# Two buffers instead of three for five small tags, in a set-attention and MoE kernel on one core

## The chip, the cores and the metric

The kernel runs on one core of a Trainium2 chip. The metric is the device time of one execution in microseconds (us), as the median of several runs. The engines that matter here are TensorE (PE, with its weight loads shown apart as PEld), ScalarE (ACT), VectorE (DVE) and SyncE's DMA queue (SPq).

## The reference

```python
def _attn_ref(x, inducing):            # x: 4 x 12480 x 128, inducing: 32 x 128
    def mab(q, kv):
        s = scale * (q @ kv.transpose(0, 2, 1))
        s = s - s.max(-1, keepdims=True)
        a = np.exp(s)
        a /= a.sum(-1, keepdims=True) + 1e-09
        return a @ kv
    h = mab(I, x)                      # I: inducing, once for each batch
    return mab(x, h)

def _moe_ref(x, w_in, w_out):          # 49920 tokens, 128 -> 2048 -> 128
    h = x @ w_in
    g = h * (1.0 / (1.0 + np.exp(-1.702 * h)))
    return g @ w_out
```

The output of the attention goes straight into the two products of the feed-forward part. The weights are handed over in 64-bit form and are decoded on the chip at the start.

## The kernel before

The work on the tokens is cut into blocks of 512. For one block the attention weights of the tokens over the 32 rows of `h` are turned and split into a high and a low part and stacked in a tile `st` (128 x 512). `h` times `w_in`, split the same way, stands in tiles `hw`. One matmul of `st` against 128 columns of `hw` so gives 128 hidden rows of a block: this is the **first product** (`hidden`, from line 1337). It is done for two chunks of hidden rows at a time, into a pair of PSUM banks `ph`. ScalarE applies the gated function to both banks in one instruction and writes `g`; ScalarE again, or VectorE by a copy, writes the rounded part `hi`, and VectorE writes the rest `lo = g - hi` (`first`, from line 1351). The **second product** (`second`, from line 1366) takes three matmuls for each chunk, and adds them up in a bank `pso`:

```python
            pe_.matmul(o, wlc, hi[:, c, :], start=(ch == 0), stop=False)
            pe_.matmul(o, whc, lo[:, c, :], start=False, stop=False)
            pe_.matmul(o, whc, hi[:, c, :], start=False, stop=last)
```

A group `i` is thus two matmuls of the first product and six of the second, all with 128 x 128 weights and 512 moving columns. A block has 8 groups, and its `pso` goes out through `ob` after the 48th matmul. There are 98 blocks' worth of such work, the last two with fewer columns (tile `left`).

The main loop (from line 1488) lays the matmuls out in one order, which is fixed when the program is built: `begin_group` decides by modelled clocks of the engines whether the next thing for TensorE is a pair of first products or three second products of an earlier group; up to 18 of those lie between the two. Pieces of the attention of later batches (`attention`, `second_softmax`, `weights_of`) are put in between, as their matmuls into banks `pa`.

The small tiles of the attention come from the pool `psm`, which has three buffers for a tag unless the tag names another number. Five tags are of interest: `mx` and `rs` (128 x 7 numbers, made once for each batch by `new_batch`, the running maxima and sums), `nmx`, `mx1` and `rs1` (128 x 1, made once for each batch, and `nmx` and `mx1` twice in the start-up, by `maximum`).

Where the tiles lie: pools are laid behind one another in each partition's memory, in the order in which they are opened, and each buffer begins at a multiple of 32 bytes. The pools for `xt`, `s1`, `e`, `aT`, `st`, `left` and `hw` are opened before `psm`, and those for `whole`/`wh`, `wl`, `g`, `hi`, `lo` and `ob` after it. The addresses in a partition, as the program of the kernel before has them:

```
tile              first address   modulo 256   part
xt                        26560          192   moving operand of the attention's products
st (4 buffers)            94016           64   moving operand of the first product
left                     102208           64   the same, for the last blocks
hw (4 buffers)           103744           64   weights of the first product
mx, rs, mx1              120128     64 to 64   (three buffers of 32 bytes for each tag)
nmx, rs1                 120544   224 to 160   (the same)
wh (2 buffers)           122848          224   weights of the second product
wl                       131040          224   weights of the second product
g (3 buffers)            139232          224
hi (9 buffers)           151520          224   moving operand of the second product
lo (9 buffers)           188384          224   moving operand of the second product
ob (2 buffers)           225248          224
```

The buffers of `st`, `hw`, `wh`, `hi` and `lo` are 2048 or 4096 bytes long and their chunks are 512 or 2048 bytes apart, so that every operand of a tag has the residue that the table gives.

Of the kernel before, what the change touches and what calls it, by code (L numbers as in the profile page):

```python
# [9 lines left out]
F32 = mybir.dt.float32  # L10
# [7 lines left out]
P = 128  # L18
# [214 lines left out]
def set_attention_then_moe(ctx: ExitStack, tc, xT, x, indT, w_in, w_out, outT):  # L233
# [67 lines left out]
    NS = len(sups)  # L301
# [11 lines left out]
    psm = ctx.enter_context(tc.tile_pool(name="psm", bufs=3))  # L313
# [49 lines left out]
    def full(some):  # L363

        free = range(len(held) - EB, len(held) - EB + sum(s < NS - 1 for s in some))
        return any(k >= 0 and not held[k] for k in free)
# [12 lines left out]
    def until(eng, t):  # L379

        while eng.t < t and not late[0]:
            yield

    def room():

        while min(dve.t, act.t) > pe_.t + ROOM and not late[0]:
            yield

    def hop(n=4):

        for _ in range(n):
            yield

    def load_xT(b, s, t=None):
        t0, g, w = sups[s]
        if t is not None:
            pass
        elif g == G:
            t = px.tile([P, SUP], F32, tag="xt", name="xt")
        else:  # L400
            t = px.tile([P, g * w], F32, tag="xt_last", name="xt_last", bufs=1)
        sp.dma_start(t[:, 0:g * w], xT[:, b * N + t0:b * N + t0 + g * w])
        xts[b, s] = t
# [24 lines left out]

    def new_batch(b):
        a = SimpleNamespace(b=b, s1={}, aTs={}, col={s: k for k, s in enumerate(EARLY + LATE if b == 0 else range(NS))})  # L430
        a.mx = psm.tile([P, NS], F32, tag="mx", name="mx")
        a.rs = psm.tile([P, NS], F32, tag="rs", name="rs")
        dve.memset(a.mx, -3.0e38)
        dve.memset(a.rs, 0.0)
        return a
# [45 lines left out]
    def max_scaled(pa):  # L481

        row = psm.tile([P, M], F32, tag="row", name="row", bufs=1)
        dve.tensor_reduce(
            row, pa[:, 0:P].rearrange("p (g m) -> p m g", g=G), axis=AX.X, op=ALU.max
        )
        dve.tensor_mul(row, row, mine)
        nmx = psm.tile([P, 1], F32, tag="nmx", name="nmx")
        dve.tensor_reduce(nmx, row, axis=AX.X, op=ALU.add)
        return nmx  # L490

# [94 lines left out]
    def pairs(some):  # L586
        some = list(some)
        return [some[k:k + 2] for k in range(0, len(some), 2)]

    def attention(b):  # L590

        for s in range(XB):
            yield from until(pe_, clocks.free("xt", XB))
            load_xT(b, s)
            yield
        a = new_batch(b)
        for pair in pairs(range(NS)):
            while full(pair):
                yield
            yield from until(  # L600
                pe_, max(clocks.ready(*[xts[b, s] for s in pair]), clocks.free("pa", 2, 2))
            )
            pas = [first_products(a, s) for s in pair]
            yield
            for s, pa in zip(pair, pas):
                if s + XB < NS:
                    load_xT(b, s + XB)
                yield from until(dve, clocks.ready(pa))
                yield from room()
                first_copy(a, s, pa, dve)  # L610
                yield from hop(HOPS[0])
            yield from hop(HOPS[1])
        mx1 = psm.tile([P, 1], F32, tag="mx1", name="mx1")
        dve.tensor_reduce(mx1, a.mx, axis=AX.X, op=ALU.max)
        yield from hop(HOPS[2])
        pa = max_everywhere(mx1)
        yield
        nmx = max_scaled(pa)
        yield from hop(HOPS[3])
        yield from until(act, clocks.ready(nmx))  # L620
        yield from deep()
        for s in range(4):
            first_exponential(a, s, nmx)
        yield
        pa = ps_a.tile([P, 512], F32, tag="pa", name="pa")
        i = 0
        xns = {}
        for s in range(XB):
            yield from until(pe_, clocks.free("xt", XB))
            xns[s] = load_x(b, s)  # L630
            yield
        for some in ((0, 1), (2, 3), tuple(range(4, NS))):
            if some[0] == 2:
                yield from deep()
                for r in range(4, NS):
                    first_exponential(a, r, nmx)
                yield
            for s in some:
                yield from until(dve, clocks.ready(a.s1[s][0]))
                yield from room()  # L640
                aT_of(a, s)
                yield from hop(HOPS[4])
            yield from until(pe_, clocks.ready(*[t for s in some for t in (a.aTs[s], xns[s])]))
            for s in some:
                i = weigh(a, pa[:, 0:P], s, xns[s], i, blocks(range(NS)))
            yield from hop(HOPS[5])
            for s in some:
                if s + XB < NS - 1:
                    xns[s + XB] = load_x(b, s + XB)
                elif s == 2:  # L650
                    t = pt.tile([P, TOK // P, P], F32, tag="t", name="xn_last")
                    xns[NS - 1] = load_x(b, NS - 1, t)
                if s != NS - 1 and s > 1:
                    again(b, s - 2)
                yield from hop(HOPS[6])
        hu = psm.tile([P, P], F32, tag="hu", name="hu", bufs=1)
        dve.tensor_copy(hu, pa[:, 0:P])
        rs1 = psm.tile([P, 1], F32, tag="rs1", name="rs1")
        dve.tensor_reduce(rs1, a.rs, axis=AX.X, op=ALU.add)
        rsb = spread(rs1)  # L660
        yield from hop(HOPS[7])
        pa = sums(hu, rsb)
        yield
        normalised(b, pa, denominators(pa[:, P:P + M]))
        yield from hop(HOPS[8])
# [164 lines left out]
    def start(pf, pw):  # L830
        a = new_batch(0)
# [170 lines left out]

        def maximum(n):
            yield dve, [a.mx], has(*[("max", s) for s in (EARLY + LATE)[:n]])
            mx1 = psm.tile([P, 1], F32, tag="mx1", name="mx1")
            dve.tensor_reduce(mx1, a.mx[:, 0:n], axis=AX.X, op=ALU.max)
            tag = "ph" if n == NS else "pa"
            yield pe_, [mx1], bank(tag)
            pa = ps_h.tile([P, 2, 512], F32, tag="ph", name="ph")[:, 0] if n == NS else None
            pa = max_everywhere(mx1, pa)  # L1010
            hold(tag)
            yield dve, [pa], None
            nmxs[n] = max_scaled(pa)
            hold(tag, -1)
            done.add(("nmx", n))
# [59 lines left out]
        def joining():  # L1075

            yield dve, lambda: [nmxs[ES], nmxs[NS]], has(("nmx", ES), ("nmx", NS), *[("exp", s) for s in EARLY])
            less = psm.tile([P, 1], F32, tag="less", name="less", bufs=1)
            dve.tensor_sub(less, nmxs[NS], nmxs[ES])
            rs1 = psm.tile([P, 1], F32, tag="rs1", name="rs1")  # L1080
            rs2 = psm.tile([P, 1], F32, tag="rs2", name="rs2", bufs=1)
            dve.tensor_reduce(rs1, a.rs[:, 0:ES], axis=AX.X, op=ALU.add)
            yield act, [less], None
            act.activation(less, less, AF.Exp)
            yield dve, [less, a.rs], has(*[("exp", s) for s in range(NS)])
            dve.tensor_reduce(rs2, a.rs[:, ES:NS], axis=AX.X, op=ALU.add)
            dve.scalar_tensor_tensor(rs1, rs1, less, rs2, op0=ALU.mult, op1=ALU.add)
            rsb = spread(rs1)
            yield pe_, [rsb], bank("pa")
            pa = ps_a.tile([P, 512], F32, tag="pa", name="pa")  # L1090
            pe_.matmul(pa[:, 0:M], rsb, rep2[:, 0:M], start=True, stop=True)
            hold("pa")
            yield dve, [pa], None
            den = denominators(pa[:, 0:M])
            hold("pa", -1)
            yield dve, [h12, less], has(*[("weighed", s) for s in range(NS)])
            hu = psm.tile([P, P], F32, tag="hu", name="hu", bufs=1)
            dve.tensor_scalar(hu, h12[:, 0:P], less, None, op0=ALU.mult)
            dve.tensor_add(hu, hu, h12[:, P:2 * P])
            yield pe_, [hu], bank("pa")  # L1100
            pa = ps_a.tile([P, 512], F32, tag="pa", name="pa")
            pe_.matmul(pa[:, 0:P], hu, rep2, start=True, stop=True)
            hold("pa")
            yield dve, [pa], None
            normalised(0, pa, den)
            hold("pa", -1)
            done.add("h")
# [447 lines left out]
```

## Time and profile before

| | before |
|---|---|
| median of 3 runs | 1568.65 us (1568.57 to 1568.71) |
| span of the profiled execution | 1566.7 us |
| TensorE busy | 1558.6 us (99%) |
| ScalarE busy | 1353.6 us (86%) |
| VectorE busy | 1309.7 us (84%) |

The span goes from the first instruction to the last one on the core; the runs' own time, with what lies around the span, is 2.0 us longer. The matmuls are pipelined: each is listed with some 0.39 us, and the next starts before it ends. What TensorE needs for one is therefore read from the distance between two starts, not from its listed length.

### The profile page before, as it was taken

How to read it: one execution, taken by the hardware profiler on the slowest of the kernel's cores; microseconds unless marked ns; L12 is line 12 of the kernel's file. 1: busy time of each engine (PE TensorE's matmuls, PEld its weight loads, DVE VectorE, ACT ScalarE, POOL GpSimd, SP SyncE). 2: the span in 40 equal slices, each digit the busy share in tenths (PEclk: the TensorE clock that was granted, in tenths of full speed). 3: DMA queues.
4: the chain of work that ended last, by engine and by line, in shares of the span. 5: the costliest groups of instructions: out<-in, count | busy, mean ns of one | idle time of the engine just before them, and what ended most of it. 6: DMA issues, size and time to landing. Idle time of an engine off the chain costs nothing.

```text
span 1566.7 us, 21731 instructions
## 1 busy us (share of the span) xinstructions
PE 1558.6 (99%) x7736; PEld 1228.8 (78%) x7736; DVE 1309.7 (84%) x1521; ACT 1353.6 (86%) x1552; POOL 4.5 (0%) x9
## 2 busy tenths in 40 slices
PE   9999999999999999999999999999999999999999
PEld 6577778877778788787787878788778888888887
DVE  7888888888888868888788887888878888888886
ACT  5999899898998898887999889888899998888884
POOL 1000000000000000000000000000000000000000
PEclk9999999999999999999999999999999999999999
DMA  8210257722151087211023119330201101101100
GB/s 328 78 44 22 58 192 125 208 62 83 29 197 41 29 150 196 73 48 61 27 91 137 38 53 220 101 95 28 68 21 40 48 24 38 48 23 39 47 23 22
DMA packets 83849, 127.53 MB, mean 81 GB/s; under 512 B 12320, under 2 KB 50848, under 8 KB 77856
## 3 DMA queue, kind: packets, MB, share of 16 engines
q1 hardware_dynamic: 83600, 126.05, 28.5%
q8 instruction: 63, 1.03, 0.3%
q14 instruction: 42, 0.34, 0.1%
q10 hardware_dynamic: 144, 0.10, 0.0%
HBM read 72.11 MB, written 25.56 MB: 62 GB/s over the span
## 4 chain that ended last, share of the span: by engine, by line
PE 97%; DMA 2%; DVE 1%; SPq 0%; issue 0%; ACT 0%; DVEq 0%
PE pso L171 69%; PE ph L171 24%; PE pa L171 4%; DMA xt<-in_xT 1%; PE h L171 0%; DVE whole L171 0%; DVE tmp L171 0%; SPq L186 0%; PE spun L1237 0%; DMA hw<-tl 0%; DVE e L171 0%; DVE s L171 0%; ACT hi L171 0%; DVE sm L171 0%; DVE tl L171 0%
## 5 line engine op out<-in xcount | busy, mean ns | idle before, releaser
L171 DVE TENSOR_TENSOR lo<-g,hi 128x1024 fp32r<-128x1024 f32 x776 | 938.4, 1217 | 155.2 <-ACT hi L171 141.7
L171 ACT ACTIVATE g<-ph 128x1024 f32<-128x1024 f32 (+1 forms) x784 | 809.8, 1036 | 177.7 <-PE ph L171 84.4
L171 PE MATMUL pso<-lo,wh 128*128 128x512 f32 (+1 forms) x1552 | 608.1, 392 | 0.0
L171 PE MATMUL pso<-hi,wl 128*128 128x512 f32 (+1 forms) x1552 | 607.6, 392 | 0.0
L171 PE MATMUL pso<-hi,wh 128*128 128x512 f32 (+1 forms) x1552 | 606.9, 391 | 0.0
L171 ACT ACTIVATE hi<-ph 128x1024 fp32r<-128x1024 f32 (+1 forms) x483 | 499.1, 1033 | 0.0
L171 PE MATMUL ph<-st,hw 128*128 128x512 f32 x1536 | 484.8, 400 | 1.4 <-ACT g L171 1.2
L171 PEld LDWEIGHTS pso<-hi,wl 128*128 128x128 f32 x1552 | 291.2, 188 | 75.7 <-issue 4.2
L171 PEld LDWEIGHTS ph<-st,hw 128*128 128x128 f32 x1536 | 285.5, 188 | 80.3 <-issue 9.0
L171 PEld LDWEIGHTS pso<-lo,wh 128*128 128x128 f32 x1552 | 291.4, 188 | 67.2 <-issue 0.2
L171 PEld LDWEIGHTS pso<-hi,wh 128*128 128x128 f32 x1552 | 291.3, 188 | 63.2
L171 DVE CAST hi<-g 128x1024 fp32r<-128x1024 f32 (+1 forms) x293 | 200.2, 683 | 76.7 <-ACT g L171 76.3
L171 ACT COPY ob<-pso 128x512 f32<-128x512 f32 (+1 forms) x98 | 59.3, 606 | 11.1 <-PE pso L171 11.1
L171 ACT ACT_TABLE_LOAD x32 | 41.1, 1283 | 1.3 <-PEq L1545 0.7
L171 PE MATMUL pa<-xt,indT_sb 128*32 128x512 f32 x200 | 24.6, 599 | 0.3 <-DMA xt<-in_xT 0.3
L171 PE MATMUL pa<-xt,hT 128*32 128x512 f32 (+1 forms) x176 | 21.5, 595 | 0.0
L171 ACT ACTIVATE s<-s,nmx 128x512 f32<-128x512 f32 (+1 forms) x27 | 17.8, 662 | 3.2 <-DVE nmx L171 3.2
L171 DVE TENSOR_SCALAR_CACHE_REDUCE s<-pa 128x512 f32<-128x512 f32 (+1 forms) x24 | 15.1, 659 | 5.7 <-PE pa L171 5.7
L171 DVE TENSOR_TENSOR e<-e,sm 128x512 f32<-128x512 f32 (+3 forms) x29 | 17.8, 613 | 1.0
L171 DVE TENSOR_REDUCE m<-e 128x16 f32<-128x512 f32 (+2 forms) x28 | 17.3, 618 | 1.0
L171 DVE STREAM_TRANSPOSE aT<-s 128x512 f32<-128x512 f32 (+1 forms) x28 | 18.0, 642 | 0.0
L171 PEld LDWEIGHTS pa<-xn,aT 128*32 128x32 f32 x576 | 15.2, 110 | 3.3 <-DVE lo L171 1.5
(125 smaller groups left out, 372.7 us busy)
## 6 DMA issues: line engine op xcount, KB each, us to landing
xt<-in_xT SPq DMA_DIRECT2D x44, 1024.0 KB, 7.0
out_T<-ob SPq DMA_DIRECT2D x96, 256.0 KB, 2.0
xn<-in_x SPq DMA_DIRECT2D x72, 256.0 KB, 8.4
st<-ahT SPq DMA_DIRECT2D x184, 64.0 KB, 2.0
st<-alT SPq DMA_DIRECT2D x184, 64.0 KB, 2.0
raw<-in_w_in SPq DMA_DIRECT2D x4, 512.0 KB, 10.8
xf<-in_x SPq DMA_DIRECT2D x2, 1024.0 KB, 17.3
raw<-in_w_out SPq DMA_DIRECT2D x4, 512.0 KB, 15.2
```

What stands on the lines that cost most here:

```text
L171: return f(*a, **k)
```

## The change

```diff
     def new_batch(b):
-        a.mx = psm.tile([P, NS], F32, tag="mx", name="mx")
-        a.rs = psm.tile([P, NS], F32, tag="rs", name="rs")
+        a.mx = psm.tile([P, NS], F32, tag="mx", name="mx", bufs=2)
+        a.rs = psm.tile([P, NS], F32, tag="rs", name="rs", bufs=2)
...
-        nmx = psm.tile([P, 1], F32, tag="nmx", name="nmx")
+        nmx = psm.tile([P, 1], F32, tag="nmx", name="nmx", bufs=2)
...
-        mx1 = psm.tile([P, 1], F32, tag="mx1", name="mx1")
+        mx1 = psm.tile([P, 1], F32, tag="mx1", name="mx1", bufs=2)
...
-        rs1 = psm.tile([P, 1], F32, tag="rs1", name="rs1")
+        rs1 = psm.tile([P, 1], F32, tag="rs1", name="rs1", bufs=2)
```

`mx1` and `rs1` are changed in the same way where the start-up makes them (`maximum`, `joining`). Each of the five tags has a buffer less, of 32 bytes: everything that lies behind `rs1` moves down by 5 x 32 = 160 bytes. `wh`, `wl`, `g`, `hi`, `lo` and `ob` then begin at 224 - 160 = 64 modulo 256, where `st` and `hw`, which don't move, already are. No instruction is added, removed or put elsewhere by the text of the diff; a buffer of the five tags comes back one batch earlier than it did.

## Rows read from the trace of the kernel before

**Rows 1.** The page: TensorE's and the others' busy time, the chain that ended last.
```profile
PE 1558.6 (99%) x7736; PEld 1228.8 (78%) x7736; DVE 1309.7 (84%) x1521; ACT 1353.6 (86%) x1552; POOL 4.5 (0%) x9
...
PE 97%; DMA 2%; DVE 1%; SPq 0%; issue 0%; ACT 0%; DVEq 0%
```

**Rows 2.** The page's costliest groups: the full-width matmuls, with busy time and mean.
```profile
L171 PE MATMUL pso<-lo,wh 128*128 128x512 f32 (+1 forms) x1552 | 608.1, 392 | 0.0
...
L171 PE MATMUL ph<-st,hw 128*128 128x512 f32 x1536 | 484.8, 400 | 1.4 <-ACT g L171 1.2
```

**Rows 3.** Timeline of TensorE, 699 to 712 us: start, length, what.
```profile
699.88 0.63 PE L171 MATMUL ph<-st,hw 128*128 128x512 f32 x2
700.35 0.39 PE L171 MATMUL pso<-hi,wl 128*128 128x512 f32 x1
700.58 0.40 PE L171 MATMUL pso<-lo,wh 128*128 128x512 f32 x1
...
710.96 0.63 PE L171 MATMUL ph<-st,hw 128*128 128x512 f32 x2
```

**Rows 4.** Timeline of TensorE, 255 to 264 us: a run without first products.
```profile
255.22 0.39 PE L171 MATMUL pso<-hi,wl 128*128 128x512 f32 x1
...
259.07 0.39 PE L171 MATMUL pso<-hi,wh 128*128 128x512 f32 x1
259.30 0.63 PE L171 MATMUL ph<-st,hw 128*128 128x512 f32 x2
259.77 0.39 PE L171 MATMUL pso<-hi,wl 128*128 128x512 f32 x1
```

**Rows 5.** Timeline of ScalarE, 276.5 to 280.5 us: the copy of a full pso.
```profile
278.45 0.58 ACT L171 COPY ob<-pso 128x512 f32<-128x512 f32 x1
```

**Rows 6.** Timeline of TensorE, 276.5 to 280.2 us: the matmuls about that copy.
```profile
277.35 0.39 PE L171 MATMUL pso<-hi,wl 128*128 128x512 f32 x1
277.57 0.39 PE L171 MATMUL pso<-lo,wh 128*128 128x512 f32 x1
277.80 0.39 PE L171 MATMUL pso<-hi,wh 128*128 128x512 f32 x1
278.03 0.39 PE L171 MATMUL pso<-hi,wl 128*128 128x512 f32 x1
278.25 0.39 PE L171 MATMUL pso<-lo,wh 128*128 128x512 f32 x1
```

**Rows 7.** Timeline of TensorE, 675 to 682 us: four first products in a row.
```profile
675.36 1.10 PE L171 MATMUL ph<-st,hw 128*128 128x512 f32 x4
676.29 0.39 PE L171 MATMUL pso<-hi,wl 128*128 128x512 f32 x1
```

**Rows 8.** Timeline of TensorE, 719.5 to 726 us: after an attention product.
```profile
722.61 1.92 PE L171 MATMUL pa<-xt,hT 128*32 128x512 f32 x16
724.46 0.50 PE L171 MATMUL pso<-hi,wl 128*128 128x512 f32 x1
724.79 0.40 PE L171 MATMUL pso<-lo,wh 128*128 128x512 f32 x1
...
725.95 0.40 PE L171 MATMUL ph<-st,hw 128*128 128x512 f32 x1
```

**Rows 9.** Waits of PE, then of PEld, 100 to 1560 us: total, times, longest.
```profile
PE ph L171 <- ACT hi L171: 0.2, 1, 0.2
...
PEld pa L171 <- issue: 19.4, 60, 0.4
...
PEld ph L171 <- ACT g L171: 4.2, 5, 0.8
```

**Rows 10.** Busy time by stretch of 20 us: PE, PEld, DVE, ACT, POOL, granted clock.
```profile
80.00:100.00 20.00, 20.00 (x88) 16.25 (x87) 17.05 (x22) 19.91 (x23) 0.00 (x0) 1.00 0.04 13
...
1120.00:1140.00 20.00, 20.00 (x88) 16.31 (x87) 15.19 (x17) 19.87 (x24) 0.00 (x0) 1.00 0.09 27
...
1340.00:1360.00 20.00, 20.00 (x88) 16.25 (x87) 17.54 (x21) 18.43 (x22) 0.00 (x0) 1.00 0.20 54
```

**Rows 11.** The instructions on mx and mx1 (one name), whole span, then 240 to 250 us.
```profile
L171 PE MATMUL ph<-ident,mx x2: 275/326/376, 27.4 to 27.7; 128*128 128x128 f32 x2
...
L171 PE MATMUL pa<-ident,mx x2: 272/274/275, 244.3 to 244.4; 128*128 128x128 f32 x2
```

More of the change, by code (lines that the diff above doesn't have):

```diff
@@ L1004, in maximum @@
             yield dve, [a.mx], has(*[("max", s) for s in (EARLY + LATE)[:n]])
-            mx1 = psm.tile([P, 1], F32, tag="mx1", name="mx1")
+            mx1 = psm.tile([P, 1], F32, tag="mx1", name="mx1", bufs=2)
             dve.tensor_reduce(mx1, a.mx[:, 0:n], axis=AX.X, op=ALU.max)
@@ L1079, in joining @@
             dve.tensor_sub(less, nmxs[NS], nmxs[ES])
-            rs1 = psm.tile([P, 1], F32, tag="rs1", name="rs1")
+            rs1 = psm.tile([P, 1], F32, tag="rs1", name="rs1", bufs=2)
             rs2 = psm.tile([P, 1], F32, tag="rs2", name="rs2", bufs=1)
```

## The prediction

> **What bounds the kernel now.** I read the page first: TensorE is busy for 1558.6 of 1566.7 us, and the chain that ended last is 97% TensorE, while ScalarE is busy for 1353.6 us and VectorE for 1309.7 us [rows 1]. The list of waits agrees: between 100 and 1560 us TensorE's matmuls wait 0.2 us for another engine, and its weight loads a few us in all [rows 9]. So the time is the number of matmuls times the distance between their starts, and the reader should look at nothing else until that distance is understood. The granted clock is 1.00 (2.4 GHz) in the stretches that I looked at [rows 10], so it isn't the clock that varies.
>
> The groups give the numbers: 1536 matmuls of the first product and 3 x 1552 of the second, all 512 columns wide but for a few [rows 2]. Their listed 0.39 to 0.40 us overlap; the timeline has the distances. In the usual beat of eight matmuls, two of the first product and six of the second, the pair at 699.88 comes back six beats later at 710.96 us: 11.08 / 6 = 1.847 us a beat, 0.2308 us a matmul [rows 3]. Where the layout sends second products alone, the distance is smaller: from 255.22 to the pair at 259.30 us there are 18 distances in 4.08 us, 0.2267 us each [rows 4]. Eight at that pace take 1.813 us. A pair of first products thus costs its beat 0.033 us more than eight second products would, although the shapes are the same.
>
> Where do the 0.033 us lie? From the pair's start to the next second product it is 0.47 us for two [rows 3, 4], 0.017 above 2 x 0.2267. So only half lies in the pair, and the rest in the second products right behind it, which wait for nobody and which, in a run of their own, go at 0.2267. The pair puts TensorE's reading out of step, and it takes some matmuls to fall in again. After an attention product it is the same: 724.79 to 725.95 us is 1.16 us for five, where 5 x 0.2267 is 1.13 [rows 8].
>
> What tells the first product from the second, then? Not the change of PSUM bank or the start of a sum: a full `pso` is copied at 278.45 us [rows 5], so the matmul at 278.03 begins the next one in another bank, and the distances about it stay 0.22, 0.23, 0.23, 0.22 [rows 6]. What is left, among the things that I can see, is where the operands lie: `st` and `hw` at 64 modulo 256, `hi`, `lo`, `wh` and `wl` at 224. That the place matters is my reading and stands in no row; the rows only leave little else.
>
> **The change, part by part.** *Instructions.* None is added or removed. The order comes from modelled clocks, in which a buffer's earlier use counts by the time when it ended. A buffer of the five tags now comes back after two tiles and not after three. The closest such return is `mx1`: the start-up's are read for the last time at 27.7 us, and the next batch's is read at 244.3 us [rows 11]. `rs1`, `nmx`, `mx` and `rs` return at like distances of a batch or two. A wait some 200 us after its event is met before it is asked, so I cost it, and the order, at nothing; its cover would have to lose 200 us to be worth a stall. If it did stall, the attention behind VectorE's instruction would be late first, and TensorE only after that.
>
> *Places.* `g` and `ob` move with the rest, but ScalarE, VectorE and the queue aren't what ends last [rows 1], so a change there is hidden by TensorE's 1558.6 us; without that cover I have no row for it, and I bound it by ScalarE's 13% of slack. The operands of the attention products keep another place (`xt` at 192), so the breaks stay.
>
> *The beat.* If equal places keep TensorE in step, each beat falls from 1.847 to 1.813 us. There are 1536 / 2 = 768 pairs [rows 2]: 768 x 0.0333 = 25.6 us. That is the upper end. The lower end, for which no row exists, is that places that all equal 64 settle at the pace of the only run at 64 that the trace has: four first products in a row, 675.36 to 676.29 us, 0.93 / 4 = 0.2325 us [rows 7], slower than now. Four is short, and the second products need as many to settle after a break [rows 8], so I take the upper end for the likeliest.
>
> *What comes off it.* (a) Weight loads of an attention product follow 60 breaks [rows 9], and about 0.027 us of falling into step (1.16 - 1.133) stays after each: 60 x 0.027 = 1.6 us. (b) ScalarE is busy for 19.9 of 20 us in two stretches [rows 10]: there a faster TensorE only waits for a bank `ph`, and 40 us x 1.8% = 0.7 us is not gained. (c) Elsewhere ScalarE has room (18.4 of 20 us at 1340 us [rows 10]), but single groups are later than that, and each wait throws TensorE out of step again. The waits of this kind that the trace has, for `g` before `ph`, are 5 with 4.2 us [rows 9]; I allow half as much again, 2 us, between 0 and 8. Sum: 25.6 - 1.6 - 0.7 - 2.0 = 21.3 us. The span would go from 1566.7 to 1545.4 us. The runs' median lies 2.0 us above the profiled span, and I keep that: 1568.65 - 21.3 = **1547.4 us**.
>
> **A rule against it.** The rows say that a matmul's distance differs by what ran before it, 0.2267 against 0.2308 [rows 3, 4]. The Trainium skill, "SBUF — State Buffer", § Who interferes with whom, gives TensorE two independent read ports, one for the moving operand and one for the weights, and says that it never waits on anyone; the same page, § Door 1, knows lines of 16 bytes, and 64 and 224 both begin one. By that page the places can't matter and the sum is zero, which is the first rival below. The trace has a difference that the page doesn't explain, so I don't take the page's side.
>
> **The rivals.**
> 1. *The place does nothing.* Then the 0.033 us belong to the first product in some way that moving the second can't mend (its two writes into two banks one after the other, say). For it: no row shows a place at work. Against it: the bank change of rows 5 and 6 costs nothing, and half of the loss sits behind the pair. The time stays at 1568.65 us, within 0.5.
> 2. *Sixty-four is the slow place* (the other side). The second products then take on the pace of the four first products. From 0.2325 up to 0.235 (with the rounding of the two starts), a beat is 1.86 to 1.88 us, 0.013 to 0.033 more than now, times 768: 10 to 25 us slower, 1579 to 1594, in the middle 1586 us. It decides as soon as the settled distance at 64 is over 0.2308 us. For it: rows 7 are the only pure run at 64, and it isn't fast. Against: second products at 224 are as slow while they settle [rows 8].
> 3. *The step is kept, but ScalarE eats half of it.* If TensorE's gain runs into ScalarE whenever that is over 90% busy, about half of the 21 us stays: 1558 us (1553 to 1564). For it: the two full stretches [rows 10]. Against: over the whole, 1353.6 of about 1545 us is 88%.
>
> **Chances and range.** The full gain 0.50 (1541 to 1553), half of it 0.13, no effect 0.13, slower 0.24. A measurement of this kernel can tell about 0.2% (3 us) from no change; faster by more than that is then 0.63, within it 0.13, slower 0.24. The range must reach past "no effect" and into the slower case: 1541 to 1582 leaves out the upper part of that case and a little below, together some 0.2.
>
> **What would show it.** Right: the same 7736 matmuls in the same order; pairs of first products 1.81 us apart in the usual beat, with eight distances that all are near 0.2267; the runs without first products as they were; breaks by attention products still followed by a few longer distances; ScalarE's share of busy time about a point higher, and some new waits of `ph` weight loads for ScalarE. Wrong in the way of rival 1: the beat still 1.847. Of rival 2: runs of second products alone, 0.2267 now, at 0.2325 or more. Of rival 3: the beat at 1.813 where TensorE runs freely, but waits for `g` or `hi` of 10 us in sum. What would make the whole argument wrong is another quantity that goes with the first product, such as its operands' places counted in more than 256 bytes, which stay unequal.

## The result, and the profile after

The changed kernel takes 1544.32 us (median of 4 runs, 1544.1 to 1545.24) against 1568.61 us of the kernel before (4 runs beside it): a ratio of 0.9846, 95% interval 0.9832 to 0.986, or 24.3 us less. The forecast was 1547.4 us, 21 us less. The profiled execution took 1544.1 us, its span is 1542.3 us.

The page of the changed kernel, beside [rows 1, 2]:

```profile
span 1542.3 us, 21731 instructions
...
PE 1533.9 (99%) x7736; PEld 1228.5 (80%) x7736; DVE 1308.9 (85%) x1521; ACT 1351.3 (88%) x1552; POOL 4.5 (0%) x9
...
L171 PE MATMUL pso<-lo,wh 128*128 128x512 f32 (+1 forms) x1552 | 602.5, 388 | 0.0
...
L171 PE MATMUL ph<-st,hw 128*128 128x512 f32 x1536 | 474.4, 393 | 1.4 <-ACT g L171 1.2
```

The counts are those of before, and the instructions of each engine stand in the same order. ScalarE and VectorE do the same work in nearly the same time, 2.3 and 0.8 us less. TensorE is busy for 24.7 us less, with the same 7736 matmuls.

The timeline of TensorE in the changed kernel, 690 to 702 us, beside [rows 3]; then four first products in a row, at 664 to 668 us, beside [rows 7]; then an attention product, at 708 to 718 us, beside [rows 8] (columns: start, length, what):

```profile
690.21 0.61 PE L171 MATMUL ph<-st,hw 128*128 128x512 f32 x2
690.66 0.39 PE L171 MATMUL pso<-hi,wl 128*128 128x512 f32 x1
690.89 0.39 PE L171 MATMUL pso<-lo,wh 128*128 128x512 f32 x1
...
701.09 0.61 PE L171 MATMUL ph<-st,hw 128*128 128x512 f32 x2
```

```profile
666.18 1.07 PE L171 MATMUL ph<-st,hw 128*128 128x512 f32 x4
667.09 0.39 PE L171 MATMUL pso<-hi,wl 128*128 128x512 f32 x1
```

```profile
712.51 1.92 PE L171 MATMUL pa<-xt,hT 128*32 128x512 f32 x16
714.37 0.50 PE L171 MATMUL pso<-hi,wl 128*128 128x512 f32 x1
714.71 0.40 PE L171 MATMUL pso<-lo,wh 128*128 128x512 f32 x1
...
715.88 0.63 PE L171 MATMUL ph<-st,hw 128*128 128x512 f32 x2
```

Six beats take 701.09 - 690.21 = 10.88 us, 1.813 each, where it was 1.847. From the pair to the next second product it is 0.45 us, 2 x 0.2267, where it was 0.47. The four first products take 0.91 us, 0.2275 each; before, 0.93. The beat now has the pace that only the runs of second products alone had. After the attention product, nothing has changed within the rounding: five distances, from 714.71 to 715.88 us, in 1.17 us, 0.04 more than 5 x 0.2267; before, 1.16.

### The profile page after: what moved, and what is told of

It is laid out like the page before. It is cut to its first block, busy times and chain, and to the rows that moved or that the text cites. A ratio compares the mean times of both kernels' runs of the same rounds, so it can differ in the third digit from the quotient of the medians.

```text
span 1542.3 us, 21731 instructions
## 1 busy us (share of the span) xinstructions
PE 1533.9 (99%) x7736; PEld 1228.5 (80%) x7736; DVE 1308.9 (85%) x1521; ACT 1351.3 (88%) x1552; POOL 4.5 (0%) x9
## 4 chain that ended last, share of the span: by engine, by line
PE 98%; DVE 1%; DMA 0%; issue 0%; SPq 0%; ACT 0%; DVEq 0%
PE pso L171 69%; PE ph L171 24%; PE pa L171 5%; PE h L171 0%; PE spun L1237 0%; DMA xt<-in_xT 0%; DVE whole L171 0%; DVE tmp L171 0%; SPq L186 0%; DMA hw<-tl 0%; DVE e L171 0%; DVE s L171 0%; ACT hi L171 0%; DVE sm L171 0%; DVE tl L171 0%
## 5 line engine op out<-in xcount | busy, mean ns | idle before, releaser
L171 PE MATMUL ph<-st,hw 128*128 128x512 f32 x1536 | 474.4, 393 | 1.4 <-ACT g L171 1.2
L171 DVE TENSOR_REDUCE sm<-e 128x16 f32<-128x512 f32 (+3 forms) x29 | 17.4, 600 | 0.4 <-ACT e L171 0.4
```

The costliest lines, as they stand in the source:

```text
L171: return f(*a, **k)
```

## The experiments

Each of them changes the place of some tiles by unused bytes (a tile that is set to zero once and never read), or by buffers that are taken away. In all twelve programs TensorE's instructions are the same and in the same order; VectorE has at most two such memsets more, near the start. The places, modulo 256, are those of the programs; xt is the attention's moving operand. The ratio is to the runs of the kernel before that were taken beside each version (medians of 1568.61 to 1568.97 us).

```
run                 xt    st, hw   wh, wl   hi, lo    time us   ratio to before (95%)
before             192        64      224      224    1568.61
after              192        64       64       64    1544.32   0.9846 (0.9832 to 0.986)
e1_back_to_224     192        64      224      224    1568.46   0.9998 (0.9989 to 1.0008)
e2_at_96           192        64       96       96    1568.41   0.9997 (0.9987 to 1.0006)
e3_at_128          192        64      128      128    1562.78   0.996  (0.9946 to 0.9975)
e4_at_192          192        64      192      192    1559.04   0.9938 (0.9923 to 0.9953)
e5_all_at_224      192       224      224      224    1544.4    0.9844 (0.983 to 0.9859)
e6_all_at_96       224        96       96       96    1544.41   0.9844 (0.9829 to 0.9858)
e7_moving_at_224   192        64       64      224    1580.03   1.0071 (1.0056 to 1.0086)
e8_weights_at_224  192        64      224       64    1582.04   1.0086 (1.0069 to 1.0103)
e9_down_256        192        64       64       64    1544.21   0.9842 (0.9829 to 0.9856)
e10_xt_too         192       192      192      192    1544.37   0.9843 (0.983 to 0.9857)
```

The first four ask whether it was the places, and by what measure they are equal. All four have the same form (40, 8, 16 and 32 numbers of padding):

```diff
     psm = ctx.enter_context(tc.tile_pool(name="psm", bufs=3))
+    pad = ctx.enter_context(tc.tile_pool(name="pad", bufs=1))
...
     ctx.enter_context(tc.manual_schedule())
+    nc.vector.memset(pad.tile([P, 40], F32, tag="pad", name="pad"), 0.0)
```

**Back to 224.** Expected: 

> The changed kernel with its two buffers, and 160 unused bytes behind the tiles of hw: the second product's operands are at 224 modulo 256 again, as before the change. Theory (the places alone did it): the time before, 1568.6 us within 1, and a beat of 1.847 us. Rival (the buffers, or what else is in the diff, did it): 1544 us.

Measured: 1568.46 us. With the two buffers and the old place, the time of before is back to within 0.1%. So neither the buffers nor the waits that they could add did anything; the whole gain is the place. `hT`, the weights of an attention product, moves with the change as well, from 96 to 192; in e1 it lies at 192 too, so it isn't what counts.

**Thirty-two bytes beside.** Expected: 

> The changed kernel with 32 unused bytes: the second product's operands at 96 modulo 256, 32 bytes beside the first's 64. Both theories of the modulus (64 or 256) expect slow: 1565 to 1570 us, a beat near 1.847 us. A theory in which only 224 is a bad place expects 1544 us.

Measured: 1568.41 us, the slow time. It isn't that 224 alone is bad. But the loss lies elsewhere in the beat than before the change, as the timeline from 690 to 700 us has it:

```profile
690.57 0.62 PE L171 MATMUL ph<-st,hw 128*128 128x512 f32 x2
691.02 0.40 PE L171 MATMUL pso<-hi,wl 128*128 128x512 f32 x1
...
692.41 0.62 PE L171 MATMUL ph<-st,hw 128*128 128x512 f32 x2
```

Here the pair and its hand-over take 0.45 us, the settled pace, and the six distances behind it 1.39 us, 0.03 over 6 x 0.2267, although those six matmuls all have their operands at 96.

**Sixty-four and 128 bytes beside.** Expected: 

> The changed kernel with 64 unused bytes: the second product's operands at 128 modulo 256, the first's at 64. If the places must be equal modulo 256 (or 128): slow, 1560 to 1570 us. If only the place modulo 64 counts: 1544.3 us within 1, a beat of 1.813 us.

> The changed kernel with 128 unused bytes: the second product's operands at 192 modulo 256, equal to the first's modulo 128 and not modulo 256. Modulo 256: slow, 1560 to 1570 us. Modulo 128 or 64: 1544.3 us within 1.

Measured: 1562.78 and 1559.04 us. The first lies in the range of modulo 256, the second 1 us below it: both are slow, so places equal modulo 64 or 128 don't do, but they are less slow than 32 bytes, which neither side had forecast. The timeline of e4_at_192, 690 to 702 us:

```profile
691.25 0.63 PE L171 MATMUL ph<-st,hw 128*128 128x512 f32 x2
691.72 0.39 PE L171 MATMUL pso<-hi,wl 128*128 128x512 f32 x1
...
692.85 0.40 PE L171 MATMUL pso<-hi,wh 128*128 128x512 f32 x1
693.09 0.63 PE L171 MATMUL ph<-st,hw 128*128 128x512 f32 x2
...
700.42 0.63 PE L171 MATMUL ph<-st,hw 128*128 128x512 f32 x2
```

Five beats in 9.17 us are 1.834 each, 0.021 over the settled 1.813. From 691.72 to 692.85 us the five distances are 0.226 each, the settled pace; the 0.021 lies about the pair (0.24 us before it, 0.47 for the pair and its hand-over). Before the change, the same five distances, from 700.35 us in [rows 3], took 1.15 us and not 1.13:

```profile
701.50 0.39 PE L171 MATMUL pso<-hi,wh 128*128 128x512 f32 x1
```

So in these beats TensorE is back at its pace right behind the pair at a distance of 128 bytes, and before the change it took a few matmuls more.

The next four ask whether 64 is a good place or equality is what counts, and whose place it is:

**All at 224.** The 160 bytes lie ahead of the tiles `st`:

```diff
     pt = ctx.enter_context(tc.tile_pool(name="pt", bufs=7))
+    pad = ctx.enter_context(tc.tile_pool(name="pad", bufs=1))
...
+    nc.vector.memset(pad.tile([P, 40], F32, tag="pad", name="pad"), 0.0)
```

Expected: 

> The changed kernel with 160 unused bytes ahead of the tiles st: first and second product both at 224 modulo 256, the attention's xt at 192 as ever. Theory (what counts is that the places are equal, wherever they are): a beat of 1.813 us and 1544 to 1547 us, the upper end if the breaks by attention products, whose operands lie 32 bytes off, are again followed by longer distances. Rival (64 is a good place in itself, 224 a bad one): 1560 us or more.

Measured: 1544.4 us, fast. Its timeline, 690 to 702 us, has the settled beat, 10.88 us for six:

```profile
690.43 0.62 PE L171 MATMUL ph<-st,hw 128*128 128x512 f32 x2
...
701.31 0.62 PE L171 MATMUL ph<-st,hw 128*128 128x512 f32 x2
```

**All at 96.** The same with 8 numbers behind the pool `const`. Expected: 

> The changed kernel with 32 unused bytes ahead of all large tiles: first and second product at 96 modulo 256, and the attention's xt at 224, so that all distances between places are those of the changed kernel. Theory (equal places, wherever): 1544.3 us within 1. Rival (a multiple of 64 is needed): 1555 us or more.

Measured: 1544.41 us, fast. Equality counts, not the place; neither a multiple of 64 nor of 128 is needed.

**The moving operand apart from the weights.** The padding lies behind `wl`:

```diff
     pwl = ctx.enter_context(tc.tile_pool(name="pwl", bufs=1))
+    pad = ctx.enter_context(tc.tile_pool(name="pad", bufs=1))
+    nc.vector.memset(pad.tile([P, 40], F32, tag="pad", name="pad"), 0.0)
```

Expected: 

> The changed kernel with 160 unused bytes behind wl: hi and lo at 224 modulo 256 again, wh and wl stay at 64 with st and hw. If the moving operands' places count: about 1568 us. If only the weights' places count: 1544 us. If both do: between, or 1568 us.

Measured: 1580.03 us, slower than before the change, which no theory had forecast. A run of second products alone, in its timeline at 256 to 268 us, shows where:

```profile
255.81 0.39 PE L171 MATMUL pso<-hi,wl 128*128 128x512 f32 x1
...
260.50 0.40 PE L171 MATMUL pso<-hi,wh 128*128 128x512 f32 x1
260.73 0.63 PE L171 MATMUL ph<-st,hw 128*128 128x512 f32 x2
```

From 255.81 to 260.73 us there are 21 distances, 0.2343 us each, and they never settle to the 0.2267 of [rows 4]. In this run nothing changes from one matmul to the next: every moving operand is at 224 and all weights are at 64.

**The weights apart from the moving operand.** The other half, with room made by fewer buffers:

```diff
-        a.mx = psm.tile([P, NS], F32, tag="mx", name="mx", bufs=2)
-        a.rs = psm.tile([P, NS], F32, tag="rs", name="rs", bufs=2)
+        a.mx = psm.tile([P, NS], F32, tag="mx", name="mx", bufs=1)
+        a.rs = psm.tile([P, NS], F32, tag="rs", name="rs", bufs=1)
...
-        m2 = psm.tile([P, BLK], F32, tag="m2", name="m2")
+        m2 = psm.tile([P, BLK], F32, tag="m2", name="m2", bufs=2)
...
     psm = ctx.enter_context(tc.tile_pool(name="psm", bufs=3))
+    pad = ctx.enter_context(tc.tile_pool(name="pad", bufs=1))
...
     pwl = ctx.enter_context(tc.tile_pool(name="pwl", bufs=1))
+    padb = ctx.enter_context(tc.tile_pool(name="padb", bufs=1))
+    nc.vector.memset(pad.tile([P, 8], F32, tag="pad", name="pad"), 0.0)
+    nc.vector.memset(padb.tile([P, 24], F32, tag="padb", name="padb"), 0.0)
```

Expected: 

> The other half: wh and wl at 224 modulo 256, hi and lo at 64 with st and hw (mx and rs have one buffer, m2 two, to make the room). If the moving operands' places count: 1544 us. If the weights' places count: about 1568 us.

Measured: 1582.04 us. A run of second products alone, at 256 to 268 us:

```profile
256.08 0.39 PE L171 MATMUL pso<-hi,wl 128*128 128x512 f32 x1
...
260.98 0.63 PE L171 MATMUL ph<-st,hw 128*128 128x512 f32 x2
```

21 distances in 4.90 us, 0.2333 each. So it isn't the one operand or the other, and again neither side of the forecast had it. What must be equal is the moving operand's place and the weights' place. No other engine holds TensorE up: all waits of its matmuls, from 100 to 1535 us, are one line, the same in e7 and e8, and that of [rows 9]:

```profile
PE ph L171 <- ACT hi L171: 0.2, 1, 0.2
```

**Is 256 the measure, and what do the last bits hold?** Two more:

```diff
 e9_down_256: one buffer for mx, rs, mx1 and rs1, two for m2 and sm, no padding
-        sm = psm.tile([P, BLK], F32, tag="sm", name="sm")
+        sm = psm.tile([P, BLK], F32, tag="sm", name="sm", bufs=2)
...
 e10_xt_too: 128 bytes behind xt
     px = ctx.enter_context(tc.tile_pool(name="px", bufs=XB))
+    pad = ctx.enter_context(tc.tile_pool(name="pad", bufs=1))
...
+    nc.vector.memset(pad.tile([P, 32], F32, tag="pad", name="pad"), 0.0)
```

Expected: 

> The changed kernel with further buffers taken away (mx, rs, mx1 and rs1 keep one, m2 and sm two), so that the second product's operands lie 256 bytes lower: 64 modulo 256 as the first's, but 64 against 320 modulo 512. If 256 is the measure: 1544.3 us within 1, which also shows that fewer buffers cost nothing. If the places must be equal modulo 512: 1555 us or more.

Measured: 1544.21 us. The second product's places differ from the first's modulo 512 and it is fast: 256 is enough. With e4_at_192, where 128 wasn't, 256 is the measure among the powers of two. Fewer buffers of the small tiles still cost nothing.

Expected: 

> The changed kernel with 128 unused bytes behind xt: all operands of both products and of the attention's xt and aT at 192 modulo 256 (hT at 64). If the longer distances after an attention product come from xt's other place: they go, about 2 us, and the time is 1542 to 1543 us. If they come from the break itself: 1544.3 us within 1.

Measured: 1544.37 us, no gain. After an attention product of this kernel, at 712 to 718 us:

```profile
712.72 1.92 PE L171 MATMUL pa<-xt,hT 128*32 128x512 f32 x16
714.58 0.50 PE L171 MATMUL pso<-hi,wl 128*128 128x512 f32 x1
714.92 0.40 PE L171 MATMUL pso<-lo,wh 128*128 128x512 f32 x1
...
716.09 0.63 PE L171 MATMUL ph<-st,hw 128*128 128x512 f32 x2
```

Five distances in 1.17 us, as with xt elsewhere. So what is lost after a break doesn't come from xt's place. That it comes with the break itself is likely and not shown: `hT` lies at 64 here, and no version has it, xt and both products at one place. No version was faster than the changed kernel by more than the runs scatter.

## Why the prediction was right

**The bound.** TensorE bounds both kernels; its busy time fell by 24.7 us and the time by 24.3.

**The instructions and the buffers.** Costed at nothing, and nothing they were: e1 has the two buffers and the time of before, and e9, with one buffer for four of the tags, is as fast as the change.

**The beat.** The step that carried the forecast was that equal places keep TensorE at the pace of [rows 4]. The beat is 1.813 us, to the third digit the pace of that run. The term of 25.6 us counted all 768 pairs alike, and they weren't. With the two traces laid side by side, matmul by matmul, 709 pairs that are followed by second products alone gained 23.5 us, 0.0332 each. The 44 pairs with other work, such as an attention product, before the next pair gained 0.6 us together, and the 15 pairs of the start-up next to nothing. That the place matters stood in no row, and the prediction said so; e1, e5 and e6 show it. The reading that pairs "put TensorE's reading out of step" was half of it. In the run of e7, where moving operands and weights each keep one place throughout, there is no step to lose, and yet the pace is 0.2343. That points to the two streams against each other. The weights of a matmul are loaded while the one before it runs; the changed kernel's timeline at 690 to 691.5 us has the load right behind the start of that matmul:

```profile
690.66 0.39 PE L171 MATMUL pso<-hi,wl 128*128 128x512 f32 x1
690.67 0.19 PEld L171 LDWEIGHTS pso<-lo,wh 128*128 128x128 f32 x1
690.89 0.39 PE L171 MATMUL pso<-lo,wh 128*128 128x512 f32 x1
```

In the kernel before, the own two operands of each matmul of the two products were equal, at 64 or at 224. What was unequal was a moving operand and the weights loaded beside it, at the two changes of a beat: into the pair and out of it. That one rule fits the order of all twelve kernels of the table: equal places of what streams and what is loaded beside it, 1544; unequal at two of eight, 1559 to 1569; unequal at six of eight, 1580 to 1582. It doesn't give the size: two changes cost a beat of the kernel before 0.034 us, and six lasting differences in e7 and e8 cost about 0.05 (beats of 1.864 and 1.867 us on average), and in e2 the loss isn't even at the two changes.

The rule was read out of the runs and not tried by itself, and a second reading fits them too: a matmul is late when its own two operands differ (e7, e8), or when a place changes from one matmul to the next (before, e1 to e4). The traces lean to the first. On average over 334 usual beats of each (all that follow another usual beat), the step from the pair to the first second product takes 0.2303 us in e7, where `st` and `wl` are equal, and 0.2350 us in e8, where they aren't. The step from the last second product to the pair takes 0.2339 us in e7, where `hi` and `hw` differ, and 0.2291 us in e8, where they are equal. That is a hint; no run separates the two readings.

**What comes off.** Term (a), the breaks, was put at 1.6 us. The 59 pairs beside breaks and in the start-up brought 0.7 us where the upper end had counted 59 x 0.0333 = 2.0, so 1.3 us came off: the size was near, though the start-up had been overlooked. Terms (b) and (c), 2.7 us for a TensorE that would wait for ScalarE, are the terms that were mis-sized: they are nothing. The stretch that was full on ScalarE, two of ScalarE's instructions in it, and the waits of weight loads, in the changed kernel (busy time by stretch, timeline, then waits from 100 to 1535 us), beside [rows 9, 10]; last, a wait of the kernel before, from 100 to 1560 us:

```profile
80.00:100.00 20.00, 20.00 (x90) 16.57 (x89) 17.15 (x21) 19.85 (x23) 0.00 (x0) 1.00 0.04 14
```

```profile
80.58 1.02 ACT L171 ACTIVATE hi<-ph 128x1024 fp32r<-128x1024 f32 x1
81.48 1.03 ACT L171 ACTIVATE g<-ph 128x1024 f32<-128x1024 f32 x1
```

```profile
PEld pa L171 <- issue: 20.7, 65, 0.4
...
PEld ph L171 <- ACT hi L171: 3.0, 6, 0.8
PEld ph L171 <- ACT g L171: 2.5, 3, 0.8
```

```profile
PEld ph L171 <- ACT hi L171: 1.3, 4, 0.7
```

ScalarE is still busy for 19.85 of 20 us, and TensorE has put 90 matmuls through the stretch where it was 88, with no idle time. A share of busy time near one was no bound here; the ScalarE instructions overlap in the listing, as the matmuls do: the one at 80.58 us is listed with 1.02 us, and the next starts 0.90 us after it. The waits for `hi` and `g` come to 3.0 + 2.5 = 5.5 us; before, they were 1.3 + 4.2 [rows 9], 5.5 as well. The new waits that the prediction looked for didn't come. So 25.6 - 1.6 = 24.0 us was the sum to make, and 24.3 was measured.

**The rivals.** *The place does nothing*: refuted by e1 beside the change. Between e1 and the change only the padding and its memset differ, and the time by 1.6%. The Trainium skill, "SBUF — State Buffer", § Who interferes with whom, calls TensorE's two read ports independent and says that TensorE never waits on anyone. As the prediction read it, the place then couldn't matter; measured, the beats differ by 1.8%. Whether it is the ports that get in each other's way no run shows. *Sixty-four is the slow place*: refuted by e5 and e6, and by the four first products at 0.2275. Yet a mechanism on that side exists: with only half of the tiles moved, e7 and e8, the kernel is 0.7 and 0.9% slower than before. *ScalarE eats half*: refuted by the 90 matmuls, and by the time.

## What to carry to other kernels

Where TensorE is the bound and its matmuls follow each other without waits, read the distances between starts, not the busy share, and compare the same shape in different company: a difference of a few nanoseconds over thousands of matmuls is some per cent. If there is one, look where the moving operands and the weights begin, modulo 256 bytes, and try to make all of them equal by a few bytes of padding. Here this cost one memset at the start (e5, e6) or, by fewer buffers, nothing. Only matmuls of this type, 128 x 128 weights and mostly 512 columns, were tried. And know that any other edit that adds or drops a small tile ahead of them moves these places, by up to 2.4% between the best and the worst here, and may be taken for the edit's own effect.

## What the runs showed of the hardware that had not been expected

- Matmuls of 512 columns with new weights each time start 0.2267 us apart when all moving operands and weights begin at equal places modulo 256 bytes (after, e5), and 0.2333 to 0.2343 us apart when these are 160 bytes apart throughout (e7, e8), at a granted clock of 1.00.
- Between products at unequal places, the loss depends on the distance: beats of 1.847 us in the kernel before, 1.834 at 128 bytes (e4), 1.813 at 0 (after, e5). By the times, 32 bytes and 160 bytes cost 24 us, 64 bytes 18 and 128 bytes 15.
- After a break TensorE needs some matmuls to reach the settled pace, at each of the places tried: 1.16 to 1.17 us for five in three kernels (before, after, e10), against 1.13. What sets this, and what the 256 bytes are in the hardware, stays open.
